# Attention with sigmoid scores and a token-mixing MLP: sums over both halves of the tensor array in one bank, under a new order

## The chip, the cores and the metric

The kernel runs on one core of one Trainium2 chip. The metric is the device time of one launch in microseconds, the median of several runs. The core has five engines that run side by side: TensorE (PE, matmuls and transposes into PSUM), VectorE (DVE), ScalarE (ACT), GpSimd (POOL) and SyncE (SP), which here only issues DMAs. PSUM has eight banks of 512 float32 per partition, 128 partitions.

## The reference

```python
def _attn_ref(q, k, v):                      # q, k, v: (8, 12, 448, 64)
    scores = scale * np.matmul(q, k.transpose(0, 1, 3, 2)) - np.log(S)
    attn = 1.0 / (1.0 + np.exp(-scores))
    return np.matmul(attn, v)

def _moe_ref(x, w_q, w_k, w_out):            # x: (8, 448, 768), from the heads side by side
    wq = x @ w_q                             # (8, 448, 64)
    wk = x @ w_k
    W_tok = scale * np.einsum('bsd,btd->bst', wq, wk)
    mixed = np.einsum('bst,btd->bsd', W_tok, x)
    return np.maximum(mixed, 0.0) @ w_out    # (8, 448, 768)
```

The scores pass through a sigmoid instead of a softmax, so no row sums are needed. The second part is linear in the token sums: the kernel forms tmp = wk^T x (64 by 768) first and then mixed = wq tmp, and never builds the 448 by 448 matrix W_tok.

## The kernel before, in words

**Attention.** The eight sequences with twelve heads each make 24 quads of four heads; quad n belongs to sequence u = n // 3. The 448 tokens of a head are split in seven blocks of 64. One scores step (function scores, line 307) takes one block: four matmuls, one on each 64 by 64 quarter of the array, put 2 x 448 scores on all 128 partitions of two neighbouring banks, and one sigmoid on ACT (L316) reads both banks and writes a bfloat16 buffer at. There are 24 x 7 = 168 such steps. A values step (L333) is four more matmuls; seven of them add up to one quad of x, transposed, which a copy (L342, or L340 in two pieces) brings to the buffers xt.

**What feeds it.** q, k and v are loaded as float32 by SP, cast to bfloat16 mostly on POOL (L192, L209, L215), and q and k are transposed, on DVE (L245, L269, L276) or on PE (L229, L237) with a copy (L294, L299). A ring of eight load buffers makes each load wait for the cast of the load eight places before it. ORDER (line 688) lists the loads; a dot moves a cast to DVE, a capital to ACT. w0 in it is the load of w_q and w_k, and w1 and w4 are the two loads of w_out, issued by POOL at line 653.

**The token MLP of a sequence.** x is transposed back on PE (tr_x: L355 with the whole array, L371 in quarters). W steps form wq and wk (mlp_wqk: L408 whole, L396 in quarters). N transposes wk (L423). U forms tmp (mlp_tmp, L437, or mlp_tmp_tiled, L452). M forms mixed and applies the relu (mlp_mix: L490, or L476 for the sequences of groups 1 and 2, whose 448 columns are laid out as 2 x 256; relu at L461 on ACT, L463 on DVE). O multiplies by w_out: out_chunk (L603, whole array, 128 tokens by 384 columns), out_pair (L522, quarters, for groups 1 and 2) and out_halves (L562, quarters). A group is two sequences; mxs[w] holds the mixed values of group w.

**Two halves of the array.** A quarter is one half of the rows (which part of the inner sum it takes) by one half of the columns (which partitions of a bank it writes). When the inner sum is split over the two row halves, each half sums into its own bank, and the two partial sums must be added. L396, L452 and L562 do that: a copy of one bank to SBUF (L403, L456, L567) and an add of the other on DVE (L404, L457, L568). out_pair avoids it in another way: each row half computes another block of tokens over the whole inner sum, in its own bank, for which it needs every row of w_out on both halves of the partitions. A second, swapped copy of w_out is made by twelve DMAs (the C steps, line 848).

**What sets the order.** Every engine runs its instructions in the order in which the program gives them; nothing reorders them. The program's order is written out by hand or by a planner: PLAN (line 132) is a string with one letter per step (S scores, P values, q and k the transposes of a quad, x, W, N, U, M, O as above, I an out_halves step, F a filling matmul, digits a cast; lower or other letters choose the engine or the form). BANKS (line 67) gives, step by step, the PSUM bank or the pair of banks that each step takes. After a step's matmuls, the copy or the sigmoid that reads its banks is issued, and the next step that is given those banks waits for it.

## Time and profile before

| what | value |
|---|---|
| time, median of 3 runs | 181.61 us (181.6 to 182.2) |
| the profiled execution's own time | 181.22 us |
| its span, first to last instruction | 179.4 us |
| busy: PE, ACT, DVE, POOL | 169.1, 158.9, 143.0, 124.2 us |
| PE weight loads busy | 115.5 us |
| mean granted clock of TensorE | 0.997 |
| bytes moved by DMA | 47.29 MB, 264 GB/s over the span |

The profile is one execution of the program, taken by the hardware profiler. Times are counted from the start of the span. L311 is line 311 of the kernel. A row of the chain gives start, length and the line that held the end at that time. A group row gives busy time, mean duration of one instruction in ns, then the idle time of the engine just before such instructions and what ended it. Matmuls overlap, so the mean duration of one (its whole way through the array) is longer than the step from one to the next; the step is what a stream costs. A row of a stretch gives the busy time of each engine in it, the granted clock and the DMA share.

### The profile page before, as it was taken

Reading aid. Unit: us, or ns where it says so; the run is one execution under the profiler, and the core shown is the slowest. Engines: PE = TensorE matmul, PEld = TensorE weight load, DVE = VectorE, ACT = ScalarE, POOL = GpSimd, SP = SyncE. Lnnn points to the kernel's source line nnn. Section 1 sums busy time; section 2 is a strip of 40 time slices with the busy share of each in tenths; the row PEclk is TensorE's granted clock in tenths of the full one; section 3 lists DMA queues with packets and bytes.
Section 4 is the critical chain, followed back from the end, with each engine's and each line's share of the span. In section 5 each row is a group of like instructions: output and inputs, shape, how many; then the busy total and the mean of one; then the engine's idle time right before and its main releaser. Section 6 shows DMA issues by size and latency. Waiting matters only on the chain.

```text
span 179.4 us, 7848 instructions
## 1 busy us (share of the span) xinstructions
PE 169.1 (94%) x3412; PEld 115.5 (64%) x3412; DVE 143.0 (80%) x223; ACT 158.9 (89%) x208; POOL 124.2 (69%) x169
## 2 busy tenths in 40 slices
PE   7888899889999999999999999999999999999990
PEld 7334545444674555755667788787888788888560
DVE  3447899998988897989999989979799885868351
ACT  4699999999999999999999999999999989967310
POOL 1286899998999999999999989879979810010000
PEclk9999999999999999999999999999999999999998
DMA  5999999999999998899996999959597432505876
GB/s 166 338 398 391 326 383 377 285 305 365 335 309 406 334 287 280 249 319 384 306 325 174 303 313 302 331 207 274 130 325 219 115 89 49 137 4 128 207 195 175
DMA packets 24914, 47.29 MB, mean 264 GB/s; under 512 B 3888, under 2 KB 18480, under 8 KB 24880
## 3 DMA queue, kind: packets, MB, share of 16 engines
q1 hardware_dynamic: 23600, 44.64, 76.9%
q0 software_dynamic: 800, 1.18, 3.6%
q10 hardware_dynamic: 480, 0.98, 1.5%
q8 instruction: 26, 0.43, 1.0%
q14 instruction: 8, 0.07, 0.1%
HBM read 35.78 MB, written 11.01 MB: 261 GB/s over the span
## 4 chain that ended last, share of the span: by engine, by line
PE 76%; ACT 15%; DMA 4%; SPq 1%; issue 1%; POOL 1%; DVE 0%
PE banks L311 16%; ACT at L316 15%; PE banks L522 15%; PE banks L333 14%; PE banks L603 13%; DMA k<-in_k_dram 4%; PE banks L562 3%; PE banks L408 3%; PE banks L371 2%; PE banks L396 2%; PE banks L355 2%; PE banks L452 2%; PE banks L476 1%; PE banks L490 1%; PE banks L437 1%
## 5 line engine op out<-in xcount | busy, mean ns | idle before, releaser
L316 ACT ACTIVATE at<-banks 128x896 bf16<-128x896 f32 x168 | 139.9, 951 | 2.9 <-PE banks L311 2.3
L311 PE MATMUL banks<-qk 64*64 64x448 bf16 x672 | 62.6, 357 | 3.7 <-ACT at L316 1.7
L333 PE MATMUL banks<-at,v 64*64 64x448 bf16 x672 | 47.3, 350 | 0.7 <-ACT at L316 0.7
L311 PEld LDWEIGHTS <-qk 64*64 64x64 bf16 x672 | 26.3, 105 | 21.4 <-issue 13.5
L522 PE MATMUL banks<-wout,mx 64*64 64x384 bf16 x672 | 36.3, 323 | 0.0
L333 PEld LDWEIGHTS <-v 64*64 64x64 bf16 x672 | 24.8, 106 | 6.7 <-issue 1.8
L342 DVE CAST xt<-banks 128x896 bf16<-128x896 f32 x22 | 23.7, 1083 | 2.4 <-PE banks L333 2.0
L522 PEld LDWEIGHTS <-mx 64*64 64x64 bf16 x672 | 23.2, 107 | 3.9 <-issue 0.2
L603 PE MATMUL banks<-wout,mx 128*128 128x384 bf16 (+1 forms) x138 | 24.4, 320 | 0.0
L192 POOL CAST qk<-k 128x896 bf16<-128x896 f32 x19 | 22.7, 1194 | 1.4 <-DMA k<-in_k_dram 1.0
L192 POOL CAST qk<-q 128x896 bf16<-128x896 f32 x18 | 21.5, 1193 | 2.5 <-DVE qk L276 1.4
L463 DVE TENSOR_SCALAR mx<-banks 128x1024 bf16<-128x1024 f32 (+3 forms) x22 | 21.3, 970 | 1.9 <-PE banks L476 0.7
L209 POOL CAST v<-v 128x896 bf16<-128x896 f32 x22 | 20.6, 950 | 1.4 <-DMA v<-in_v_dram 0.9
L603 PEld LDWEIGHTS <-mx 128*128 128x128 bf16 x138 | 12.3, 98 | 9.7 <-issue 3.2
L161 POOL COPY swap<-qk 32x448 uint32<-32x448 uint32 x28 | 15.5, 554 | 2.3 <-DVE qk L192 0.7
L276 DVE STREAM_TRANSPOSE qk<-qk 128x448 f32<-128x448 f32 x28 | 17.0, 628 | 0.1
L164 POOL COPY qk<-qk 32x448 uint32<-32x448 uint32 x28 | 15.8, 566 | 1.6
L167 POOL COPY qk<-swap 32x448 uint32<-32x448 uint32 x28 | 15.4, 552 | 1.6
L245 DVE STREAM_TRANSPOSE qk<-qk 32x448 f32<-32x448 f32 x24 | 15.3, 636 | 0.6
L405 POOL COPY wq<-wqk 64x448 bf16<-64x448 bf16 x3 | 1.7, 554 | 15.7 <-DVE wqk L404 15.7
L636 DVE COPY o<-banks 128x384 f32<-128x384 f32 x12 | 6.6, 554 | 5.7 <-PE banks L603 5.3
L636 ACT COPY o<-banks 128x384 f32<-128x384 f32 x9 | 4.4, 490 | 7.1 <-PE banks L603 6.6
(87 smaller groups left out, 207.9 us busy)
## 6 DMA issues: line engine op xcount, KB each, us to landing
q<-in_q_dram SPq DMA_DIRECT2D x24, 448.0 KB, 6.6
v<-in_v_dram SPq DMA_DIRECT2D x24, 448.0 KB, 6.6
k<-in_k_dram SPq DMA_DIRECT2D x23, 448.0 KB, 7.6
out_dram<-o SPq DMA_DIRECT2D x50, 192.0 KB, 4.2
wout<-in_moe_w_out_dram POOLq DMA_DIRECT2D x2, 576.0 KB, 11.7
wout<-wout SPq DMA_DIRECT2D x12, 96.0 KB, 5.6
out_dram<-o ACTq DMA_DIRECT2D x4, 192.0 KB, 3.2
k<-in_k_dram SPq DMA_DIRECT2D x1, 256.0 KB, 4.8
```

The source lines that it names most:

```text
L161: eng.tensor_copy(out=z[lo], in_=w[hi, 0])
L164: eng.tensor_copy(out=w[hi, 0], in_=w[lo, 1])
L192: COPY[e](out=f[:, :, "qk".index(nm)].rearrange("p e i d y -> p e y i d"), in_=ld.pop((nm, n)).rearrange("p (y i e d) -> p e y i d", y=2, ...
L209: COPY[e](out=t16.rearrange("p b i d -> p (b i d)"), in_=ld.pop((nm, n)).rearrange("p b x -> p (b x)"),)
L276: nc.vector.transpose(out=qk[n][:, t].rearrange("p t i n -> p (t i n)").bitcast(F32), in_=w)
L311: nc.tensor.matmul(sc[HALF[h], g, 0:S], qk[n][HALF[g], h, 1, i, :], qk[n][HALF[g], h, 0].rearrange("p i n -> p (i n)"), start=True, stop=True,
L316: inst = nc.scalar.activation(at, sc[:, :, 0:S], ACTF.Sigmoid, bias=attn_bias, scale=attn_scale)
L333: nc.tensor.matmul(ps[HALF[g], h, 0:S], ld["v16", n][HALF[h], g, i, :], ats[n, i][HALF[h], g, :], start=(i == 0), stop=(i == NI - 1),)
L342: read(fb, COPY[eng](out=xt(u, j)[:, :, 0:S], in_=ps[:, :, 0:S]))
L463: inst = nc.vector.tensor_scalar(dst, ps, moe_scale, 0.0, ALU.mult, ALU.max)
L522: nc.tensor.matmul(ps[HALF[x], y, 0:NB], mx[HALF[y], u, b, 64 * (i - 3 * y) : 64 * (i - 3 * y) + 64], wout16[HALF[y], slot(y, b), x * NB : ...
L603: nc.tensor.matmul(ps, mxs[w][:, 2 * S * c + m * P : 2 * S * c + (m + 1) * P], wout16[:, c, w0:w1], start=(c == 0), stop=(c == NC - 1),)
```

## The change

The partial sums no longer meet in an add. In the three places where the inner sum is split over the row halves (wq and wk, tmp, and the output), the columns or token blocks are now split in two as well, one for each bank. In the first half of the step, row half y sums its part into bank y; in the second half, row half y sums its part of the other block into bank 1 - y, onto what the other row half has left there. At the end each bank holds a finished sum, and one copy over both banks brings it out. Between the halves no two row halves may write one bank at the same time, so TensorE waits until its own last matmul of the first half is done (change). PLAN places other steps between the two halves; a letter V is added for the second half of tmp.

With it out_pair, the second copy of w_out and its twelve DMAs go, and the 2 x 256 layout of groups 1 and 2. The pool of output tiles has four buffers instead of three, there are 20 buffers at instead of 16, and wout16 is half as large. PLAN, BANKS and ORDER are new throughout; the group of two sequences, the functions for scores, values and transposes, and the loads themselves are the same. By the built programs PE has 3546 matmuls instead of 3412, and 25 waits on its own matmuls: 3 for wq and wk, 4 for tmp, 18 for the output.

```diff
-    p_o = pool("o", 3)
+    p_o = pool("o", 4)
...
+    SYNC = mybir.DependencyInfo(mybir.DependencyClass.Sync, mybir.DependencyReason.DATA)
+    turned = {}
+
+    def change(key):
+
+        tc.add_manual_dep(
+            nc.tensor.nop().ins, turned.pop(key).ins.name, SYNC, reason="the halves of the array change banks",
+        )
...
-    wout16 = singles.tile([P, 2 * NC, D], BF16, name="wout16")
+    wout16 = singles.tile([P, NC, D], BF16, name="wout16")
...
-    at_bufs = [singles.tile([P, 2, S], BF16, name=f"at{n}") for n in range(16)]
+    at_bufs = [singles.tile([P, 2, S], BF16, name=f"at{n}") for n in range(20)]
...
     def mlp_wqk(u, c, tail, act, tiled):
...
         if tiled:
-            for y in range(2):
-                for x in range(2):
-                    nc.tensor.matmul(
-                        ps[HALF[x], y, 0:S], wqk16[HALF[y], c, 64 * x : 64 * x + 64],
-                        xt(u, c // 2)[HALF[y], c % 2, 0:S], start=(c == 0), stop=(c == NC - 1),
-                    )
+            z, j = divmod(c, NJ)
+            if c == NJ:
+                change("W")
+            for b in (2 * j, 2 * j + 1):
+                for y in range(2):
+                    for x in range(2):
+                        inst = nc.tensor.matmul(
+                            ps[HALF[x], y ^ z, 0 : S // 2], wqk16[HALF[y], b, 64 * x : 64 * x + 64],
+                            xt(u, j)[HALF[y], b % 2, (y ^ z) * S // 2 : (y ^ z) * S // 2 + S // 2],
+                            start=(z == b == 0), stop=(z == 1 and b == NC - 1),
+                        )
+            if c == NJ - 1:
+                turned["W"] = inst
             if c == NC - 1:
-                part = p_one.tile([P, S], F32, tag="wpart", name="wpart")
-                read(fb, COPY["s" if act else "v"](out=part, in_=ps[:, 0, 0:S]))
-                read(fb, nc.vector.tensor_tensor(out=w[:, 0:S], in0=ps[:, 1, 0:S], in1=part, op=ALU.add))
-                nc.gpsimd.tensor_copy(out=w2[HALF[1]], in_=w[HALF[0], 0:S])
+                src = ps[:, :, 0 : S // 2]
+                read(fb, nc.vector.tensor_copy(out=w[:, 0:S].rearrange("p (z s) -> p z s", z=2), in_=src))
...
-    def mlp_tmp_tiled(u, act):
+    def mlp_tmp_tiled(u, t, act):
...
+                z = r ^ t
                 for y in range(2):
-                    nc.tensor.matmul(
-                        ps[HALF[y], r, 0:NB], wkn[u][HALF[r], m, :], xns[u][HALF[r], m, y * NB : (y + 1) * NB],
-                        start=(m == 0), stop=(m == 3 - r),
+                    inst = nc.tensor.matmul(
+                        ps[HALF[y], z, 0:h], wkn[u][HALF[r], m, :],
+                        xns[u][HALF[r], m, y * NB + z * h : y * NB + z * h + h],
+                        start=(t == m == 0), stop=(t == 1 and m == 3 - r),
                     )
-        read(fb, COPY["s" if act else "v"](out=part, in_=ps[:, 0, 0:NB]))
-        read(fb, nc.vector.tensor_tensor(out=tmps[u], in0=ps[:, 1, 0:NB], in1=part, op=ALU.add))
+        if t == 0:
+            turned["T"] = inst
+            return
+        read(fb, COPY["s" if act else "v"](
+            out=tmps[u].rearrange("p (z x) -> p z x", z=2), in_=ps[:, :, 0:h],
+        ))
...
-    def out_pair(act, split):
...
-    def out_halves(act):
+    def out_halves(act, split):
...
+        z, h = divmod(part, 2)
+        if part == 2:
+            change("O")
         for c in range(3 * h, 3 * h + 3):
-            t0 = 2 * S * c + m * P + b * NP
             for y in range(2):
+                t0 = 2 * S * c + m * P + (y ^ z) * NP
                 for x in range(2):
-                    nc.tensor.matmul(
-                        ps[HALF[x], y, 0:NB], mxs[w][HALF[y], t0 : t0 + NP], wout16[HALF[y], c, x * NB : (x + 1) * NB],
-                        start=(c == 0), stop=(c == NC - 1),
+                    inst = nc.tensor.matmul(
+                        ps[HALF[x], y ^ z, 0:NB], mxs[w][HALF[y], t0 : t0 + NP],
+                        wout16[HALF[y], c, x * NB : (x + 1) * NB],
+                        start=(part == 0 and c == 0), stop=(z == 1 and c == NC - 1),
                     )
-        if h:
-            read(fb, COPY["s" if act else "v"](out=o[:, b], in_=ps[:, 0, 0:NB]), keep=True)
-            read(fb, nc.vector.tensor_tensor(out=o[:, b], in0=ps[:, 1, 0:NB], in1=o[:, b], op=ALU.add), keep=True)
+        if part == 1:
+            turned["O"] = inst
...
+        if split:
+            for b in range(2):
+                read(fb, COPY["vs"[b]](out=o[:, b], in_=ps[:, b, 0:NB]), keep=True)
+        else:
+            read(fb, COPY["s" if act else "v"](out=o, in_=ps[:, :, 0:NB]), keep=True)
...
     ORDER = (
-        "q1 k1 k2 q2 q3 v0 w2 k3 v1 k4 q4 v2 w0 k5 q5 w1 v3 W5 v4 q6 k6 w4 k7 v5 q7 v6 q8 k8 k9 "
+        "q1 k1 v0 .q2 q3 k2 k3 v1 w0 q4 W3 v2 k4 v3 k5 w6 q5 q6 k6 k7 v4 w1 q7 w4 v5 k8 v6 q8 v7 "
...
-        elif kind == "C":
-            for y in range(2):
-                nc.sync.dma_start(out=wout16[HALF[y], NC + c, :], in_=wout16[HALF[1 - y], c, :])
```

More of the change, by code (lines that the diff above doesn't have):

```diff
@@ L384, in tr_x @@
             read(fb, COPY["vs"[g] if tail else eng](out=dst, in_=src))
-    wkn, tmps, mxs = {}, {}, {}
+    wkn, tmps, mxs, pt = {}, {}, {}, {}
     pw = {}
@@ L441, in mlp_tmp @@
         read(fb, COPY["s" if act else "v"](out=tmps[u], in_=ps))
-    def mlp_tmp_tiled(u, act):
-        tmps[u] = p_one.tile([P, NB], BF16, tag="tmp", name="tmp")
-        part = p_one.tile([P, NB], F32, tag="upart", name="upart")
-        fb, ps, _ = bank2()
+    def mlp_tmp_tiled(u, t, act):
+        h = NB // 2
+        if t == 0:
+            tmps[u] = p_one.tile([P, NB], BF16, tag="tmp", name="tmp")
+            pt[0] = bank2()
+        else:
+            change("T")
+        fb, ps, _ = pt[0]
         for m in range(4):
@@ L845 @@
             mlp_wqk(*divmod(c, NC), tail, t in "wl", t in "Ll")
-        elif kind == "C":
-            for y in range(2):
-                nc.sync.dma_start(out=wout16[HALF[y], NC + c, :], in_=wout16[HALF[1 - y], c, :])
         elif kind == "N":
@@ L851 @@
         elif kind == "U":
-            (mlp_tmp_tiled if t in "Tt" else mlp_tmp)(c, t in "ut")
+            tiled[c] = t if t in "Tt" else None
+            if tiled[c]:
+                mlp_tmp_tiled(c, 0, False)
+            else:
+                mlp_tmp(c, t == "u")
+        elif kind == "V":
+            if tiled[c]:
+                mlp_tmp_tiled(c, 1, tiled[c] == "t")
         elif kind == "M":
```

110 lines of the change are left out of this document (27 added, 83 removed), and 28 rows, old and new, of tables (BANKS, ORDER).

## The prediction

> **What bounds the kernel now.** I read four views in this order: the busy times of the engines in stretches of the span, the chain that ended last, the groups by line and shape, and the timeline of single engines where a latency was wanted.
>
> ```profile
> core 0: us, PE busy (x) PEld busy (x) DVE busy (x) ACT busy (x) POOL busy (x), PEclk, DMA share, GB/s
> 10.00:40.00 30.00, 26.36 (x510) 14.05 (x511) 26.28 (x36) 29.91 (x38) 26.68 (x33) 1.00 1.08 351
> 40.00:70.00 30.00, 29.57 (x538) 16.84 (x534) 26.80 (x41) 29.31 (x37) 27.66 (x39) 1.00 1.01 336
> 70.00:100.00 30.00, 30.00 (x513) 19.40 (x511) 26.84 (x39) 29.43 (x39) 28.42 (x38) 1.00 0.88 292
> 100.00:130.00 30.00, 29.92 (x731) 24.20 (x732) 26.39 (x40) 29.39 (x39) 26.08 (x37) 1.00 0.83 263
> 130.00:150.00 20.00, 20.00 (x552) 16.51 (x546) 17.57 (x23) 19.48 (x25) 12.29 (x18) 1.00 0.57 169
> 150.00:165.00 15.00, 15.00 (x444) 12.89 (x436) 10.52 (x21) 12.46 (x22) 0.56 (x1) 1.00 0.34 83
> ```
>
> Two engines stand at their limit. ACT is busy 29.91 us of the 30 between 10 and 40 us and, adding the rows, 137.52 of the 140 us from 10 to 150: it idles 2.48 us there. PE has gaps until 40 us and then 124.49 busy us of 125 up to 165. A busy PE need not be one that streams at its full rate, so I looked at single runs of matmuls in the chain.
>
> ```profile
> 11.49 27.67 ACT at L316 x34
> ...
> 46.46 1.08 PE banks L603 x6
> 47.55 0.31 PE banks L311 x4
> ...
> 52.86 0.57 PE banks L333 x12
> ...
> 57.12 0.77 PE banks L437 x8
> ...
> 80.09 0.98 PE banks L603 x6
> ...
> 100.40 0.45 PE banks L355 x8
> ...
> 102.64 0.57 PE banks L452 x14
> ...
> 111.49 0.49 PE banks L522 x12
> ...
> 158.94 0.25 PE banks L371 x32
> ```
>
> The chain runs through 34 sigmoids from 11.49 to 39.16 us (27.67 / 34 = 0.814 us each) and from there over PE. The runs repeat: four matmuls on the quarters of the array take 0.57 / 3 = 0.19 us for 448 columns and 0.49 / 3 = 0.163 us for 384; a matmul on the whole array takes 0.98 / 6 = 0.163 us for 384. Width sets the price, and nothing is left between neighbours of one shape. What is left lies at a change of shape: six L603 matmuls take 1.08 us behind quarters against 0.98 behind another whole-array line, and four L311 matmuls behind them 0.31 against 0.19. A switch of shape so costs 0.10 to 0.12 us, and I take 0.11. So from 40 us on the end moves with PE's work, and ACT stands right behind it with 2.5 us of room.
>
> **The change part by part, PE.** I counted matmuls and switches in the built order of both kernels.
>
> - Output projection: quarter matmuls of 384 columns go from 816 (L522 and L562) to 864, whole-array ones (L603) from 138 to 126. That is +48 x 0.49/12 = +1.96 and -12 x 0.163 = -1.96: nothing.
> - Mixing: groups 1 and 2 lose the padding to 512 columns. Twelve steps of eight 256-column matmuls become steps of four 448-column ones. The first kind takes 0.21 us, from start to the next line's start:
>
> ```profile
> 95.10 0.30 PE L476 MATMUL banks<-wq,tmp 64*64 64x256 bf16 x2
> ...
> 95.31 0.68 PE L522 MATMUL banks<-wout,mx 64*64 64x384 bf16 x12
> ```
>
>  12 x (0.19 - 0.21) = -0.24 us.
> - The sum over tokens (tmp): one tiled step fewer (14 matmuls of 384 columns, 0.57 us; the other four keep their columns in 28 half-wide matmuls), one untiled step more (eight L437 matmuls, 0.77 less its switch = 0.66): +0.09.
> - The tiled projections to wq and wk keep their columns in twice as many matmuls: 0. Bounds: nothing shows a 224 or 192 column matmul, but 64, 256, 384 and 448 columns cost 0.25/32, 0.21/8, 0.49/12 and 0.57/12 us, so 7.8, 26, 41 and 47.5 ns, in proportion to width within 15%. Half-wide ones could thus be dearer by at most 15% of about 5.7 us, 0.8; I take 0, since the neighbours on both sides (64 and 256 columns) are near proportion.
> - Transposes of x: one quad goes from L355 to L371: 0.25 - 0.45 = -0.20.
> - Switches of shape: 68 become 63: -5 x 0.11 = -0.55.
>
> Sum: -0.24 + 0.09 - 0.20 - 0.55 = -0.90 us.
>
> The row of 32 transposes in 0.25 us is one matmul in 7.8 ns: on quarters of the array no floor shows above that. The Trainium skill, "TensorE: Matmul & The Clock Gate", section "Wait — 56ns, not 53.3ns?", speaks against narrow matmuls: start to start never falls below about 25 ns, however few the columns. By it the sum would be, as an estimate from that page, some 0.7 us higher; the trace does not bear it out.
>
> **The waits on PE's own matmul.** There are 25: three for wq and wk, four for tmp, 18 for the output halves. Both halves of the array may not write one bank at once, so the first matmul after the change waits for the last one before it. No row shows PE waiting for itself, so I bound it. Uncovered, the price is the matmul's time past its own streaming, and the way from a signal to the next matmul:
>
> ```profile
> L522 PE MATMUL banks<-wout,mx 64*64 64x384 bf16 x672 | 36.3, 323 | 0.0
> ```
>
> ```profile
> 161.01 0.81 PE L452 MATMUL banks<-xn,wkn 64*64 64x384 bf16 x14
> 161.86 0.48 ACT L456 COPY upart<-banks 128x384 f32<-128x384 f32 x1 [0.81 <-PE banks L452]
> 162.38 0.56 DVE L457 TENSOR_TENSOR tmp<-banks,upart 128x384 bf16<-128x384 f32 x1
> ...
> 162.99 0.11 PEld L490 LDWEIGHTS <-tmp 64*64 64x64 bf16 x4
> 163.05 0.35 PE L490 MATMUL banks<-wq,tmp 64*64 64x448 bf16 x2
> ```
>
> 323 - 163 = 160 ns past streaming, 40 ns from PE's end (161.82) to a reader, and 110 ns from a finished producer (162.94) to PE's next matmul: 0.27 us together with the larger of the two signals. Bounds: 0 and 25 x 0.27 = 6.8 us. In the built order other PE work stands in each of the 25 places: in one it is a single step of scores (0.19 us), in one 32 transposes (0.25), in the other 23 two steps or more (0.35 and up). That covers 0.27 us in 23 places and leaves 0.08 + 0.02 = 0.1 us. I take 0.1. Behind each waiting instruction stand scores that ACT needs, which is why the cover counts.
>
> **What else moves.** DVE loses the adds that joined the two halves; it is not the bound (26.8 of 30 us at its fullest), so I cost its relief at nothing, and at nothing the larger pools. SP loses the twelve copies of w_out (the diff's C steps); by the windows above PE has 0.5 us of gaps in the 125 us from 40 us on, so there is nothing to win there either. ACT gets more before its last sigmoid:
>
> ```profile
> L636 ACT COPY o<-banks 128x384 f32<-128x384 f32 x9 | 4.4, 490 | 7.1 <-PE banks L603 6.6 <-ACT mx L461 0.4 <-ACT at L316 0.2
> L461 ACT ACTIVATE mx<-banks 128x448 bf16<-128x448 f32 x6 | 3.2, 564 | 0.2 <-PE banks L490 0.2
> L461 ACT ACTIVATE mx<-banks 128x1024 bf16<-128x1024 f32 x2 | 2.0, 1018 | 0.0
> L535 ACT COPY o<-banks 128x768 f32<-128x768 f32 x2 | 1.6, 798 | 0.6 <-PE banks L522 0.6
> L340 ACT CAST xt<-banks 128x448 bf16<-128x448 f32 x2 | 1.1, 561 | 0.0
> L209 ACT CAST v<-v 128x896 bf16<-128x896 f32 x1 | 0.9, 930 | 0.0
> ```
>
> Before: nine 384-wide copies (4.41), one 768-wide (0.80), one L340 (0.56), two 1024-wide relus (2.04), two narrower ones (priced at the 448 row: 1.13), one v cast (0.93): 9.9 us. After: eight copies of 384 (3.92), one of 768 (0.80), three L340 (1.68), three relus of 448 (1.69), one v cast (0.93), and three of 896 columns out of the banks, for which I take 0.93 between 0.80 and 1.02 (2.79): 11.8 us. So +1.9 us, against 2.48 us of idle: the room shrinks to 0.6 us but is not gone.
>
> **Sum.** -0.90 + 0.1 = -0.8 us against the profiled execution's own 181.22 us (179.4 of span and 1.8 around it): 180.4. That execution lies 0.4 us under the median, and I forecast for the median: 181.6 - 0.8 = 180.8; as the lighter DVE can only release banks sooner, I round to **180.7**.
>
> **The rivals.**
>
> A, ACT eats the gain (the change shortens PE, and nothing follows). If ACT keeps its 2.48 us of idle, its last sigmoid starts 1.9 us later.
>
> ```profile
> 6.44 5.97 ACT L316 ACTIVATE at<-banks 128x896 bf16<-128x896 f32 x7 [0.80 <-PE banks L311]
> ...
> 152.20 3.35 ACT L316 ACTIVATE at<-banks 128x896 bf16<-128x896 f32 x4
> ```
>
> These are the first seven and the last four. Behind the last scores PE's order gets shorter: 48 fewer quarter matmuls of the output (-1.96), 32 fewer transposes (-0.25), four more values matmuls (+0.19), an untiled tmp for a tiled one (+0.09) and two switches (+0.22): -1.7 us. So +1.9 - 1.7 = +0.2: 181.8. For it: ACT is at 98% for 140 us. Against it: part of ACT's idle time is waiting for late scores, which come sooner.
>
> B, both streams close up. If ACT's idle time halves (-1.2), A becomes -1.0, and if it vanishes -2.3: about 179.5. For it: a lighter DVE; against it: two engines that both stand at their limit rarely interlock without gaps.
>
> C, slower: a load that comes late where ACT has no room. The place is the third quad: its k is now the ninth load and must be cast on POOL, transposed on PE and copied by DVE before the 15th sigmoid.
>
> ```profile
> 9.14 0.93 POOL L215 CAST k<-k 128x896 bf16<-128x896 f32 x1 [0.23 <-DMA k<-in_k_dram]
> ...
> 13.86 0.93 POOL L209 CAST v<-v 128x896 bf16<-128x896 f32 x1 [0.19 <-DMA v<-in_v_dram]
> ```
>
> ```profile
> 17.37 1.09 DVE L299 COPY qk<-banks 128x1792 bf16<-128x1792 bf16 x1 [0.87 <-PE banks L229]
> ```
>
> The ninth load is there at about 13.8 us (the v cast waited for it), the cast ends at 14.8, transposes and copy (0.3 + 1.09, and 0.2 of signals) at 16.4. The seventh sigmoid ends at 12.41 (6.44 + 5.97) and starts, by the chain, at 11.49, so the 15th is due at 11.49 + 8 x 0.814 = 18.0, and its scores 0.4 us ahead, at 17.6. The room is 1.2 us; what is later goes to the end one for one, since ACT is full until 150 us. It decides from 1.2 + 0.8 = 2.0 us late; at 3.2 us late: 181.6 - 0.8 + 2.0 = 182.8. For it: POOL waited 0.2 us for the load in both rows, so nothing is in hand there. Against it: 1.2 us of room.
>
> D, slower: the cover of the self-waits fails, say because PE's queue holds nothing ahead of the wait. 25 x 0.27 - 0.9 = +5.9: 187.5; it turns the sign from four open places of 25. Against it: the order above.
>
> E, narrow matmuls have a floor. If a half-wide one costs no less than the 256-column one (26 ns by its row), 144 x 2.2 + 112 x 5.6 ns = 0.95 us are added and the gain is gone: 181.7. For it speaks no row, against it the transposes. This is the rule of the Trainium skill that is named above ("TensorE: Matmul & The Clock Gate").
>
> **How the numbers follow.** A measurement here can tell about 0.5%, 0.9 us, from no change: faster is under 180.7, slower over 182.5. The forecast (from 179.9 to 181.3) has 0.42, split 0.25 faster and 0.17 same, as its middle lies at the bound; A 0.20 (same); B 0.14 (faster); C 0.15 (0.12 slower, 0.03 same); D 0.07 (slower); E 0.02 (same). Faster 0.39, same 0.42, slower 0.19. The range takes in B, the forecast, A, E and C up to some 3.5 us late, and leaves out D and the far ends of B and C: 179.2 to 183.3.
>
> **What would show it.** PE's work: a run of twelve output matmuls at 0.49 us on both sides of a change, and 63 switches at 0.1. The self-waits: PE idle before the changed line, under its releaser PE, summing to about 0.1 us; several us would be D. A: ACT's idle time between 10 and 150 us as before, with the last sigmoid later than 154.7 us and PE's tail behind it 1.7 us shorter. C: sigmoids 14 to 22 with gaps that a load or a cast ended. E: half-wide matmuls at 25 ns each. I would be wrong altogether if PE waited for DVE or POOL between 40 and 150 us, where before it hardly waits.

## The result, and the profile after

The changed kernel takes 183.41 us (median of 22 runs, 181.86 to 185.69), the kernel before in the same comparison 181.89 us (22 runs, 180.73 to 184.08). The ratio is 1.0084 with a 95% interval from 1.0057 to 1.011: slower by about 1.5 us, where 0.9 us less was forecast. The medians are over all runs, the ratios leave disturbed runs out, so a ratio need not be the quotient of its medians. The profiled execution of the changed kernel took 184.2 us, with a span of 182.4 us.

First the busy times in the same stretches as before:

```profile
core 0: us, PE busy (x) PEld busy (x) DVE busy (x) ACT busy (x) POOL busy (x), PEclk, DMA share, GB/s
10.00:40.00 30.00, 25.65 (x531) 14.26 (x531) 24.20 (x34) 29.84 (x37) 26.27 (x32) 1.00 1.03 357
40.00:70.00 30.00, 28.51 (x555) 18.21 (x553) 27.00 (x40) 29.04 (x37) 27.95 (x38) 1.00 0.92 277
70.00:100.00 30.00, 29.91 (x588) 18.70 (x577) 27.17 (x41) 29.41 (x38) 28.13 (x38) 1.00 0.93 323
100.00:130.00 30.00, 29.67 (x671) 21.36 (x669) 23.83 (x35) 29.83 (x41) 25.93 (x37) 1.00 0.82 260
130.00:150.00 20.00, 18.98 (x560) 15.91 (x562) 14.66 (x22) 18.19 (x23) 10.11 (x16) 1.00 0.55 148
150.00:165.00 15.00, 15.00 (x462) 12.02 (x456) 8.68 (x17) 13.75 (x22) 0.55 (x1) 1.00 0.35 83
```

Between 40 and 150 us PE idles 1.49 + 0.09 + 0.33 + 1.02 = 2.93 us; before it was 0.43 + 0 + 0.08 + 0 = 0.51. These 2.4 us and a first sigmoid at 7.08 instead of 6.44 us (a difference that comes and goes: 6.2 to 7.1 us in the other profiles of the new order, but for the one with more warm-ups) add up to the 3.0 us by which the span is longer. It is no full account: the stretch from the first to the 43rd sigmoid also takes 34.59 us instead of 34.13, and PE has less work by shape. The chain that ended last names two places:

```profile
35.21 0.57 issue
35.78 0.90 POOL wout L633
36.67 1.09 POOL qk L200
37.77 14.37 DMA wout<-in_moe_w_out_dram
52.18 0.68 PE banks L536 x12
...
111.15 0.38 PE banks L319 x8
...
113.17 0.49 PE banks L536 x12
...
123.55 0.38 PE banks L411 x16
...
129.67 1.35 issue
131.02 0.32 PE banks L379 x17
```

**L, a late load.** Before, the chain ran through 34 sigmoids up to 39 us and then over PE. Now it runs through a load: the second half of w_out is issued by GpSimd at 37.77 us (at 30.86 before), lands 14.37 us later (12.81 before), and PE's output matmuls wait for it. **F, a late packet of instructions.** At 129.67 us PE stands still for 1.35 us and waits for nothing that the profile shows, in the middle of a run of 32 transposes (15 before the gap, 17 behind it). The timeline of PE shows both in brackets:

```profile
52.18 0.68 PE L536 MATMUL banks<-wout,mx 64*64 64x384 bf16 x12 [0.84 <-DMA wout<-in_moe_w_out_dram]
```

```profile
129.31 0.36 PE L379 MATMUL banks<-ident,xt 64*64 64x64 bf16 x15
131.02 0.32 PE L379 MATMUL banks<-ident,xt 64*64 64x64 bf16 x17 [1.35 <-issue]
```

Why instructions? PE's instructions reach it by DMA, in packets. The view of the DMA queues has a row for that queue, first of the kernel before, then of the changed one:

```profile
q8 instruction: 26, 0.43, 1.0%
```

```profile
q8 instruction: 27, 0.44, 1.0%
```

0.44 MB in 27 packets is some 16 kB each. By the built program the transpose behind the gap is PE's instruction number 4803, and 4803 = 18 x 256 + 195. The other gaps marked "issue" that are quoted below sit at numbers with that rest too. So I take a packet for 256 instructions (64 bytes each), and its first one for a border. PE has 7101 instructions now against 6833.

### The profile page after: what moved, and what is told of

Read it like the earlier page. It is cut to its first block, busy times and chain, and to the rows that moved or that the text cites. A ratio compares the mean times of both kernels' runs of the same rounds, so it can differ in the third digit from the quotient of the medians.

```text
span 182.4 us, 8090 instructions
## 1 busy us (share of the span) xinstructions
PE 169.7 (93%) x3546; PEld 114.2 (63%) x3546; DVE 134.8 (74%) x212; ACT 160.2 (88%) x209; POOL 120.6 (66%) x165
## 4 chain that ended last, share of the span: by engine, by line
PE 67%; DMA 20%; POOL 6%; DVE 2%; issue 2%; SPq 1%; POOLq 0%; DVEq 0%
PE banks L536 19%; PE banks L319 13%; PE banks L341 12%; PE banks L583 11%; DMA wout<-in_moe_w_out_dram 8%; DMA v<-in_v_dram 4%; DMA k<-in_k_dram 4%; DMA w<-in_moe_w_k_dram 4%; POOL qk L200 3%; PE banks L503 2%; PE banks L427 2%; PE banks L411 2%; PE banks L379 2%; PE banks L363 1%; PE banks L455 1%
## 5 line engine op out<-in xcount | busy, mean ns | idle before, releaser
L536 PE MATMUL banks<-wout,mx 64*64 64x384 bf16 x864 | 45.8, 323 | 0.8 <-DMA wout<-in_moe_w_out_dram 0.8
L319 PEld LDWEIGHTS <-qk 64*64 64x64 bf16 x672 | 27.4, 105 | 20.1 <-issue 9.7
L536 PEld LDWEIGHTS <-mx 64*64 64x64 bf16 x864 | 28.8, 107 | 7.3 <-issue 1.4
L341 PEld LDWEIGHTS <-v 64*64 64x64 bf16 x672 | 23.1, 106 | 7.4 <-issue 1.5
L492 DVE TENSOR_SCALAR mx<-banks 128x896 bf16<-128x896 f32 (+1 forms) x23 | 20.4, 902 | 4.7 <-PE banks L503 4.5
L350 DVE CAST xt<-banks 128x896 bf16<-128x896 f32 x17 | 18.5, 1087 | 6.2 <-PE banks L341 6.1
L583 PE MATMUL banks<-wout,mx 128*128 128x384 bf16 (+1 forms) x126 | 21.6, 319 | 0.0
L200 POOL CAST qk<-k 128x896 bf16<-128x896 f32 x17 | 20.3, 1195 | 1.0 <-DVE qk L284 0.4
L175 POOL COPY qk<-swap 32x448 uint32<-32x448 uint32 x28 | 15.9, 569 | 1.6
L551 DVE COPY o<-banks 128x768 f32<-128x768 f32 x11 | 10.5, 950 | 4.7 <-PE banks L536 2.9
L392 DVE COPY xn<-banks 128x1024 bf16<-128x1024 bf16 (+1 forms) x15 | 9.7, 647 | 4.0 <-PE banks L379 3.7
```

The lines of the kernel that those rows point to most:

```text
L175: eng.tensor_copy(out=w[lo, 1], in_=z[lo])
L200: COPY[e](out=f[:, :, "qk".index(nm)].rearrange("p e i d y -> p e y i d"), in_=ld.pop((nm, n)).rearrange("p (y i e d) -> p e y i d", y=2, ...
L319: nc.tensor.matmul(sc[HALF[h], g, 0:S], qk[n][HALF[g], h, 1, i, :], qk[n][HALF[g], h, 0].rearrange("p i n -> p (i n)"), start=True, stop=True,
L341: nc.tensor.matmul(ps[HALF[g], h, 0:S], ld["v16", n][HALF[h], g, i, :], ats[n, i][HALF[h], g, :], start=(i == 0), stop=(i == NI - 1),)
L350: read(fb, COPY[eng](out=xt(u, j)[:, :, 0:S], in_=ps[:, :, 0:S]))
L492: inst = nc.vector.tensor_scalar(dst, ps, moe_scale, 0.0, ALU.mult, ALU.max)
```

## The experiments

Three theories about the 1.5 us. **L**: the late w_out load. **F**: the late packet. **Cover**: part of the PE work that was saved lay ahead of 40 us, where ACT sets the pace, so nothing is gained there. A rival to all of them is that the self-waits or the half-wide matmuls cost more than priced. The times of before differ a little from chip to chip, so each ratio is taken on one chip; the changed kernel's is 1.0084, and ratios, not medians, are what to compare across paragraphs. The diffs of ORDER show only the part of the line that changes.

**The load earlier, and the waits without cover.** The first edit moves the two w_out loads in ORDER:

```diff
-  v3 k5 w6 q5 q6 k6 k7 v4 w1 q7 w4 v5
+  v3 w1 k5 w6 q5 w4 q6 k6 k7 v4 q7 v5
```

> The changed kernel with one edit: in the list of loads the two loads of w_out are issued by POOL some 8 us earlier. Theory L (the loads of w_out come late: in the changed kernel's profile PE stands 0.84 us and ACT 0.76 us at the first output step, behind a load that took 14.4 us): that idle time is gone, the stretch from 45 to 60 us is 0.8 to 1.2 us shorter, and the time lies some 1.0 us under the changed kernel, 182.2 to 182.6. Rival W (the waits of PE on its own matmuls make the loss): time as the changed kernel, 183.2 to 183.6. Rival F (a packet of PE's instructions comes late, 1.35 us once in the profile): as the changed kernel on average, with a gap of PE at an instruction number that leaves the rest 195 when divided by 256.

Measured: 183.87 us, ratio 1.0122 [1.0075, 1.0168]. The wait at 52 us is gone from the profile (PE is busy 10.00 of the 10 us from 50 to 60), the gap at 130 us stays with 0.89 us, and the time doesn't fall, where some 1.0 us less was expected. The 35th sigmoid comes 0.5 us late under this order, so the edit isn't a clean test of L.

The second edit puts each `change` right behind the last matmul that it waits for, so that nothing covers the wait.

```diff
-            if c == NJ:
-                change("W")
...
             if c == NJ - 1:
                 turned["W"] = inst
+                change("W")
```

> The changed kernel with the 25 waits of PE on its own matmul set right behind that matmul, so that no other PE work covers them. By the prediction's price each costs 0.27 us, and where PE is the bound they add up: 25 x 0.27 = 6.8 us, some 190 us; those that fall where ACT is the bound cost less, so 188 to 190. Rival W (the waits cost much already where they stand): only a little is added, 183.5 to 185.

Measured: 188.3 us, ratio 1.035 [1.0297, 1.0403]. At a bared wait mostly 0.38 to 0.40 us pass from the start of the last 384-column matmul to the next start, where four such matmuls take 0.16 us without a wait; behind half-wide ones it is 0.30 to 0.32 us against 0.08 to 0.10. So a wait costs some 0.24 us, an estimate from these starts. The waits view names PE as its own releaser, up to 0.5 us a time; then that view of the changed kernel, which has one such row:

```profile
PEld L319 <- PE banks L532: 3.1, 7, 0.4
PEld L501 <- PE banks L532: 2.2, 5, 0.4
```

```profile
PEld L476 <- PE banks L476: 0.2, 1, 0.2
```

Uncovered, the waits cost 4.6 us more than the changed kernel took on the same chip (183.71, below); covered, the changed kernel's profile has 0.2 us of them. They aren't the cause.

**Both kernels again.** To see what is constant, the changed kernel and the one before ran unchanged.

> The changed kernel itself, a second profile. Theory L: the stand at the first output step shows again, 0.5 to 1.2 us, at the same place. Rival F: a gap of PE behind a late packet of instructions shows in some executions and at varying places; the 1.35 us at 129.6 us need not come again. Time 183.0 to 184.0.

> The kernel before, a second profile. Theory L: no wait of PE for the loads of w_out, which are issued 15 us ahead of their first use. Rival F: gaps of PE of 0.3 us and more at the same rest of the instruction number, if any. The first sigmoid starts within 0.7 us of the 6.4 us of the first profile, which tells how far the 0.65 us later start of the changed kernel's profile is its own.

Measured: 183.71 us, ratio 1.007 [1.0019, 1.012], and 180.91 us for the one execution of the kernel before. The second profile of the changed kernel has the wait for w_out again, larger, and two gaps for want of instructions, at numbers 4803 and 5315:

```profile
52.28 0.68 PE L536 MATMUL banks<-wout,mx 64*64 64x384 bf16 x12 [1.71 <-DMA wout<-in_moe_w_out_dram]
```

```profile
130.59 0.32 PE L379 MATMUL banks<-ident,xt 64*64 64x64 bf16 x17 [0.62 <-issue]
141.33 0.54 PE L341 MATMUL banks<-at,v 64*64 64x448 bf16 x5 [1.67 <-issue]
```

The places recur, the sizes vary. That this makes single executions spread by over 3 us is not shown: those of the kernel before spread as much, and in its two profiles PE has neither that wait nor a gap over 0.35 us after 40 us.

**The borders moved by 96 instructions.** 48 more warm-up matmuls (with their weight loads 96 instructions) ahead of everything:

```diff
-    for _ in range(32):
+    for _ in range(80):
```

> The changed kernel with 80 instead of 32 warm-up matmuls, which run while PE waits for the first loads (about 2.7 us of 4): 96 more PE instructions ahead of everything else, and nothing else changed. Theory F (PE's instructions arrive in blocks of 256, and a block that is used up too fast leaves PE waiting for the next): the block borders stand 96 instructions earlier in the work, where three blocks hold only 2.3 to 3.4 us of PE work; gaps without a releaser stand again at instruction numbers with the rest 195 by 256, at other places of the work than 129.6 us, and are larger: 185 to 188 us. Theory L and rival W (late load of w_out, waits on own matmuls): nothing changes but the start, 183.2 to 184.0.

Measured: 184.92 us, ratio 1.0169 [1.0105, 1.0232]. The warm-ups start the first sigmoid 2 us late (8.64 us). The gap in the transposes is gone: no row of PE's timeline from 119 to 145 us ends in "issue". Less these 2 us (0.011 of the ratio) it is 1.006, within the noise of the changed kernel's 1.0084. The larger gaps that the expectation names elsewhere don't come: 0.25 us at 163.39 us is all.

**The inner projections as before.** The tiled wq and wk steps and tmp go back to full-width matmuls in two banks, with a copy and an add (seven waits and 128 matmuls fewer); once with the w_out loads late, once with them early as in the first edit, and the early loads alone once more.

```diff
-                            ps[HALF[x], y ^ z, 0 : S // 2], wqk16[HALF[y], b, 64 * x : 64 * x + 64],
+                        ps[HALF[x], y, 0:S], wqk16[HALF[y], c, 64 * x : 64 * x + 64],
...
+                read(fb, nc.vector.tensor_tensor(out=w[:, 0:S], in0=ps[:, 1, 0:S], in1=part, op=ALU.add))
```

> The changed kernel with two of its three new sums undone: wq and wk, and tmp, are again summed in full-width matmuls in two banks and joined by a copy and an add; the output halves, the order and the banks stay. 128 fewer matmuls, 256 fewer PE instructions (a whole block), 7 of the 25 waits gone, the same columns, 7 copies and adds more on DVE. Theory F: the gap at 129.6 us shrinks or goes, 0.5 to 1.2 us less than the changed kernel: 182.3 to 183.0. If only the late w_out counts: 183.2 to 183.6, or a little more for the adds.

> The last kernel with the loads of w_out issued earlier as well. Theories L and F together: both gaps gone, 181.3 to 182.0, at the kernel before or a little under it. Theory F alone: as the last kernel.

> The changed kernel with the loads of w_out issued earlier, once more with more rounds, since six timed runs showed no gain (183.87) while the profile showed the stand at the first output step gone (2.33 us of PE gaps between 40 and 70 us against 3.55 and 4.2). Theory L: 182.3 to 182.9 in the median. If the gap that goes there only comes back later (ACT or instruction packets): 183.4 to 184.0, with gaps after 70 us larger by about 1 us than in the changed kernel's profiles.

Measured: 183.3 us, 1.0076 [1.0038, 1.0115]; 183.15 us, 1.0077 [1.0039, 1.0115]; 183.6 us, 1.0118 [1.0062, 1.0174]. So the half-wide matmuls and the waits are about even with the full-wide ones and their adds. With 256 PE instructions fewer the first two profiles have no gap for want of instructions from 119 to 145 us (the third has 1.37 us at 129.67 us), yet the load's wait is there again in the first of the three:

```profile
52.49 0.68 PE L522 MATMUL banks<-wout,mx 64*64 64x384 bf16 x12 [1.22 <-DMA wout<-in_moe_w_out_dram]
```

The second has neither L nor that gap, was expected at 181.3 to 182.0 us, and is no faster than the first. This speaks against L and F as the whole cause in the median.

**One projection as before, and fillers in pieces.** A smaller shift: only group 5's wq and wk in full-width matmuls, 48 instructions fewer ahead of 130 us. And a shift without delay: each of the ten filler matmuls of 512 columns is cut into six, 100 instructions more.

```diff
+        if tiled and u == 5:
...
+                        ps[HALF[x], y, 0:S], wqk16[HALF[y], c, 64 * x : 64 * x + 64],
...
+            return
```

```diff
-            nc.tensor.matmul(bank1()[1], zeros[:, 0:P], zeros, start=True, stop=True)
+            filled = bank1()[1]
+            for y in range(6):
+                cut = slice(86 * y, min(86 * y + 86, 512))
+                nc.tensor.matmul(filled[:, cut], zeros[:, 0:P], zeros[:, cut], start=True, stop=True)
```

> Only the projection to wq and wk of group 5 goes back to full-width matmuls in two banks, a copy and an add: 24 matmuls (48 instructions of PE, with their weight loads) and one self-wait fewer, ahead of 130 us. Late packet of PE's instructions: the gap of 1.35 us in the middle of the transposes at 131 us shrinks or is gone, because PE reaches the border 48 instructions later in its stream and with more time since the last packet; 0.6 to 1.0 us less than the changed kernel, 182.4 to 182.8. Saved PE work lies under ACT's cover, and that is all: no difference, 183.4. DVE's add and the extra bank cost: 0 to 0.3 us more, 183.4 to 183.7.

> The changed kernel with each of the filler matmuls of 512 columns ahead of the first scores cut into six: the same columns, 100 instructions of PE more, all borders between packets of PE's instructions fall 100 instructions earlier in the work, and the start isn't delayed. Late packet: the gap in the transposes at 131 us moves to a place where PE is slower between two borders and is hidden there; 0.6 to 1.3 us less, 182.1 to 182.8. Cover of ACT alone: no difference, 183.4 within 0.3. If the borders that the fillers move fall badly elsewhere: up to 184.5, with an issue gap at another place of the stream.

Measured: 183.67 us, 1.0078 [1.0031, 1.0126], and 184.07 us, 1.0159 [1.0112, 1.0206]. In both profiles the "issue" gap in the transposes at 131 us is gone. The first has the largest wait for w_out so far, 2.12 us at 52.55 us. The second has none, but new gaps, each at a border (instructions 1731, 1987 and 2755):

```profile
51.38 0.35 PE L319 MATMUL banks<-qk 64*64 64x448 bf16 x1 [0.80 <-issue]
57.58 0.64 PE L536 MATMUL banks<-wout,mx 64*64 64x384 bf16 x9 [0.17 <-issue]
78.06 0.38 PE L319 MATMUL banks<-qk 64*64 64x448 bf16 x3 [0.75 <-issue]
```

Moving the borders moves the gaps; it doesn't end them.

**More PE work, early and late.** Twelve scores steps are issued twice, the second time over the first.

```diff
+        for _ in range(2 if 20 <= len(sigmoids) < 32 else 1):
...
+        for _ in range(2 if 100 <= len(sigmoids) < 112 else 1):
```

> The changed kernel with the scores of the 21st to 32nd step issued twice (the second time over the first, so the output is the same): 12 x 0.19 = 2.3 us more work for PE while ACT is dense, 20 to 33 us. Theory that PE's work ahead of 40 us lies under ACT's cover: the sigmoids of these steps keep their 0.81 us and the time rises by under 0.8 us, to 183.4 to 184.2. The prediction's ledger, by which every microsecond of PE's work reaches the end: 2.3 us more, 185.7.

> The same repetition for the 101st to 112th step, around 100 to 112 us, again 12 x 0.19 = 2.3 us more work for PE. There PE is the bound by the windows: both theories expect all of it at the end, 185.5 to 185.9 (less by up to 0.8 if the 96 more instructions also move the border of the late packet at 131 us to a better place, 184.7). If it also stays under 184.2, ACT's cover reaches the whole program and the ledger fails everywhere.

Measured: 185.66 us, 1.0241 [1.0169, 1.0313], and 183.65 us, 1.0133 [1.0082, 1.0185], four runs each. The early repetition, then the late one, in the stretch from 20 to 34 us:

```profile
20.00:34.00 14.00, 13.19 (x252) 7.08 (x247) 11.34 (x18) 13.24 (x17) 13.38 (x17) 1.00 1.03 385
```

```profile
20.00:34.00 14.00, 12.60 (x290) 7.33 (x290) 12.43 (x20) 14.00 (x19) 13.30 (x19) 1.00 1.00 371
```

ACT loses 0.76 us of its 14 to 2.3 us of extra PE work, and after 43 sigmoids, counted from the first, the early kernel is 35.29 - 33.93 = 1.36 us behind. So by the trace 0.9 to 1.5 us of 2.3 were covered (2.3 less 1.36 and less 0.76): the cover is partial. The measured times don't show it: by the ratios, against 1.0084, the early repetition costs some 2.9 us, more than its work, and the late one, expected at its full 2.3, some 0.9. Behind the early repetition the profile has a gap of 1.09 us at 78.26 us for want of instructions, where the changed kernel has none. The late repetition, beside the changed kernel's trace, costs 1.9 us from the 97th to the 115th sigmoid and gets 1.5 of it back from the 139th to the 145th: its 96 instructions move the border out of the transposes at 131 us, and the gap there is gone. But 183.65 us also lies under the 184.2 at which the expectation gives up the ledger of PE's work everywhere. A plain addition of work and a shift of borders can't be had apart here, so Cover stays open.

**The loads behind q5, alone and with the shift; later loads; the kernel before with cut fillers.**

In ORDER, first behind q5 (once alone and once with group 5 as before), then later:

```diff
-  q5 q6 k6 k7 v4 w1 q7 w4 v5
+  q5 w1 w4 q6 k6 k7 v4 q7 v5
```

```diff
-  q5 q6 k6 k7 v4 w1 q7 w4 v5
+  q5 q6 k6 k7 v4 q7 v5 w1 w4
```

The kernel before gets the same cut of its filler matmuls as above.

> The changed kernel with both w_out loads issued on GpSimd right behind the cast of q5, at about 30 us instead of 35.8 and 37.8; nothing else moves ahead of q5 and k5, so the 36th sigmoid isn't late as it was in the earlier version. L (PE and ACT wait at 52 us for w_out): the gap at 52 us is gone, 1.0 us less than the changed kernel, 182.2 to 182.6, with the late packet at 131 us left. F alone: no difference, 183.4.

> Both edits: the loads behind q5, and the projection to wq and wk of group 5 in full-width matmuls. L and F together are the cause: 181.6 to 182.3, the time of before within 0.3%, both gaps gone and PE's last matmul at about 175 us. If the early part (PE idle under ACT up to 43 sigmoids, 0.9 us more than before) is a loss too and not only missing gain: 182.5. Neither L nor F: 183.4 to 183.7.

> The changed kernel with both w_out loads issued behind the cast of v5, about 3 us later than in the changed kernel. L: the loads land about 2 to 3 us later, PE waits at 52 us for that much longer, and the time rises by 1.5 to 3 us, 184.9 to 186.4. If the wait at 52 us is in the profiled execution only or is made good later: 183.4.

> The kernel before with each of its filler matmuls cut into six, which moves all borders between packets of PE's instructions by 100. If a random place of the borders costs about what it costs in the changed kernel, and the order of before has a good one: 0.5 to 1.3 us more, 182.4 to 183.2, with an issue gap in PE's stream that before doesn't have. If late packets cost nothing at before's density of instructions (6833 against 7101): no difference, 181.9.

Measured: 183.57 us, 1.0088 [1.005, 1.0125]; 182.6 us, 1.0044 [1.0002, 1.0086]; 189.11 us, 1.0293 [1.0209, 1.0377]; 182.51 us, 1.0023 [0.9986, 1.0059].

The later loads are the strongest sign for L. They were issued at 37.34 and 38.2 us, only 1.6 and 0.4 us later than in the changed kernel (my 3 us was wrong), back to back; the second took 15.9 us, landed 2.0 us later than in the changed kernel, and PE waited 4.06 us. The measured time rose by some 3.8 us by the ratios (5.7 between the medians, which are of two chips):

```profile
54.20 1.18 PE L536 MATMUL banks<-wout,mx 64*64 64x384 bf16 x12 [4.06 <-DMA wout<-in_moe_w_out_dram]
```

The wait isn't all of it. From 50 to 60 us, behind the two longest waits (4.06 us here, 2.12 in the kernel with only group 5 as before, above), TensorE's mean granted clock (the third number from the end) is 0.66 and 0.83; in the changed kernel's second profile, with a wait of 1.71 us, it stays at 1.00:

```profile
50.00:60.00 10.00, 5.94 (x72) 3.93 (x71) 3.34 (x5) 3.64 (x5) 9.28 (x15) 0.66 0.95 335
```

```profile
50.00:60.00 10.00, 7.88 (x142) 5.79 (x139) 5.26 (x8) 6.48 (x9) 9.28 (x15) 0.83 0.93 336
```

```profile
50.00:60.00 10.00, 8.29 (x188) 6.37 (x184) 7.24 (x10) 8.33 (x12) 9.29 (x14) 1.00 0.95 347
```

For the same work, between the 43rd and the 97th sigmoid, PE is busy 48.80 and 47.60 us there, and 45.82 in the changed kernel's first profile. So the low clock adds 3.0 and 1.8 us to the wait itself. The kernel with the later loads also has a packet's gap of 1.91 us at 136.37 us.

With the loads behind q5 that wait is gone, and 1.11 us at 129.39 us is left of F; with group 5 as before, 0.37 us of it:

```profile
129.39 0.32 PE L379 MATMUL banks<-ident,xt 64*64 64x64 bf16 x17 [1.11 <-issue]
```

```profile
129.34 1.46 PE L547 MATMUL banks<-wout,mx 64*64 64x384 bf16 x29 [0.37 <-issue]
```

The two differ by 0.97 us in the measured median, the way that F would have it, but their intervals overlap. And the kernel before, its borders moved, has in its profile what it never had:

```profile
122.00 0.76 PE L396 MATMUL banks<-xt,wqk 64*64 64x448 bf16 x11 [1.71 <-issue]
```

```profile
138.37 0.35 PE L311 MATMUL banks<-qk 64*64 64x448 bf16 x1 [1.11 <-issue]
```

These sit at instructions 4291 and 5059. So the gaps are no property of the new matmuls: the order of before has borders in harmless places. Its measured time hardly moves, though: the profile is of one of its longest executions (185.21 of 182.04 to 185.55 us), so such gaps need not be in the median one.

**The place behind k7.** Behind q5 the loads (1.67 us on GpSimd) push the casts of q6 and k6 back, PE waits 0.42 and 0.47 us for them (in the kernel with group 5 as before), and the 35th sigmoid comes 0.83 us late. (The expectation puts this down to the copy of wq, which was late too; the trace names the casts.) So they stand behind k7 in the last two.

```diff
-  q5 q6 k6 k7 v4 w1 q7 w4 v5
+  q5 q6 k6 k7 w1 w4 v4 q7 v5
```

> Both edits as in the run before, but the w_out loads stand behind the cast of k7, after GpSimd's copy of wq, issued at 34.9 and 35.8 us instead of 30.8 and 31.7. L and F explain the slowdown and the late copy explains what was left: 181.6 to 182.2, within 0.3% of before, no gap over 0.3 us at 52 or 131 us and the 35th sigmoid on time. If the loads then still land after 51 us (14 to 16 us after their issue, as in the kernels with late loads): a gap of 0.3 to 0.8 us at 51 us and 182.4 to 183. If the early part under ACT's cover costs by itself: 182.6 as before.

> The place behind k7 alone, on the changed kernel: L smaller or gone, no late copy of wq, the late packet at 131 us (F) stays. With F at 1.0 us by the pair of runs behind q5: 182.6 to 183.1. If F's 1.0 was chance: 181.8 to 182.3, as the run beside it.

Measured: with group 5 as before 182.65 us, 1.0056 [1.0024, 1.0089]; without 183.16 us, 1.0075 [1.0034, 1.0117]. No wait for w_out is left in either. In the first the 35th sigmoid is on time, PE idles 0.05 us from 40 to 70 us, and what is left of its idle time is mostly F:

```profile
100.00:130.00 30.00, 29.30 (x677) 21.92 (x679) 24.46 (x36) 28.62 (x38) 24.27 (x36) 1.00 0.81 253
130.00:150.00 20.00, 19.82 (x561) 16.19 (x557) 13.81 (x19) 19.35 (x25) 10.56 (x16) 1.00 0.56 148
```

```profile
128.93 1.46 PE L547 MATMUL banks<-wout,mx 64*64 64x384 bf16 x29 [0.67 <-issue]
```

From start to start of its matmuls PE takes 0.99, 0.45 and 0.31 us at three borders here (at 128.9, 143.1 and 147.1 us). Its span is still 1.0 us longer than that of the kernel before, and PE's idle time from 40 to 150 us only 0.5 us longer (1.02 against 0.51): the other half has no name here.

**What this adds up to.** Both edits together may bring back up to half: 1.0044 and 1.0056 against 1.0084, but 1.0077 where all inner projections are as before, and all three intervals overlap the changed kernel's. One edit alone brings nothing that can be measured: without L 1.0122, 1.0118, 1.0088 and 1.0075, with F shifted alone 1.0078 and 1.0076. That the load and the packets stall PE is shown by the profiles, and for the load by its later place too; how much either costs the median execution isn't, and so the cause of the 1.5 us is shown for the profiled executions only.

Profiled executions with the late load mostly lie above the median of their kernel (up to 2.3 us), those with the early one 0.4 to 1.0 us below it, so the wait may be longer in the profiled executions than in the others. No trace shows an unprofiled one, and that stays open. Known of each execution is its mean granted clock: it is 0.991 or less, as in the two profiles above, in 25 of 152 executions of the new order (all 6 with the later loads, 2 of the changed kernel's first 22) and in 1 of 105 of the kernel before. So a halved clock goes with the new order, but it is too rare to make the difference of the medians. No version here beats the kernel before.

## Why the prediction was wrong, point by point

- **The prices of PE's work** held. Twelve output matmuls take 0.49 us, sixteen half-wide L411 ones 0.38 us (23.8 ns each, half of 47.5), twelve of 192 columns 0.25 us (L476, 20.8 ns), eight of 448 columns in the mixing 0.38 us. Rival E's price, 26 ns for a half-wide matmul, is refuted by these rows. The floor of about 25 ns that the Trainium skill gives in "TensorE: Matmul & The Clock Gate", section "Wait — 56ns, not 53.3ns?", is not, for one quarter: the starts come in groups of four, one on each quarter, and the groups stand 83 ns apart for 192 columns (0.25 us / 3) and 31 for 64 (0.25 / 8). Only the mean over the four quarters falls below 25 ns. By these prices and the counts of the prediction PE's work is some 0.85 us less than before, against 0.90 predicted:

```profile
123.55 0.38 PE banks L411 x16
...
134.00 0.25 PE banks L476 x12
...
166.77 0.38 PE banks L503 x8
```

- **The self-waits** held: 0.1 us predicted, one row of 0.2 us seen; the price of 0.27 us came out at some 0.24 where they were bared. Rival D didn't happen.
- **ACT's extra work** was sized right (copies of 896 columns at 0.93 us; measured 0.92 and 0.97), and it wasn't what decided:

```profile
L350 ACT CAST xt<-banks 128x896 bf16<-128x896 f32 x2 | 1.9, 971 | 0.0
...
L490 ACT ACTIVATE mx<-banks 128x896 bf16<-128x896 f32 x1 | 0.9, 919 | 0.0
```

 ACT idles 3.69 us from 10 to 150 us against 2.48, waiting where PE waits. The last sigmoid starts at 158.97 us, 4.4 us later and not A's 1.9; from there to the start of PE's last matmul it is 18.97 us against 20.33, so 1.4 us less, near A's 1.7.
- **"From 40 us on the end moves with PE's work"** is doubtful as a way to book the 0.9 us. Some of it may have been saved ahead of 40 us, where ACT is at 29.84 of 30. PE's busy time from 10 to 40 us falls by 0.71 us (26.36 to 25.65), but the first sigmoid starts 0.64 us later, and from the first to the 43rd it falls only from 29.79 to 29.68. The early repetition's trace has 0.9 to 1.5 of 2.3 us covered, its measured time none. How much of the gain was lost in this way isn't shown.
- **"What else moves"** is the step that failed worst. I counted the twelve copies of w_out that go, and costed the loads at nothing. The two loads of w_out themselves had moved behind v4 and q7 in ORDER, 9.3 and 6.9 us later, against a use at 50 to 51 us and landings 11.1 and 14.4 us after the issue (10.7 and 12.8 before). PE's 0.5 us of gaps after 40 us, which I read as "nothing to win there", said nothing of what there was to lose: they became 2.93 us in the profile, 0.84 of them for this load, which is nearly the whole gain that was forecast.
- **The supply of instructions** had no term at all. Twice as many half-wide matmuls at the same streaming cost are 268 instructions of PE more, and a gap of this kind stood in the trace of before, at instruction 1731, where I passed it over (the row below). In the profile of the changed kernel it is 1.35 us, and with the load's 0.84 it makes the larger part of the 2.4 us of idle time that came new; whether both do as much in the median execution stays open:

```profile
54.31 0.57 PE L311 MATMUL banks<-qk 64*64 64x448 bf16 x7 [0.35 <-issue]
```

- **Rival C** named the right kind, a load that comes late where there is no room, and its 182.8 us was the nearest forecast, partly by luck: the place was wrong. Its own place, early in the program, does show up, one cast further on: in four of 17 profiles of the new order the load of k3 holds GpSimd up, v1's cast stands behind it, and PE waits for v1 for 0.94 to 1.44 us. The kernel with the loads behind k7 alone has it:

```profile
16.38 1.19 POOL L200 CAST qk<-k 128x896 bf16<-128x896 f32 x1 [1.65 <-DMA k<-in_k_dram]
17.69 0.94 POOL L217 CAST v<-v 128x896 bf16<-128x896 f32 x1
```

```profile
18.68 0.96 PE L341 MATMUL banks<-at,v 64*64 64x448 bf16 x8 [1.44 <-POOL v L217]
```

 In the three profiles of the order of before it doesn't occur. It is perhaps part of the spread, and of what both edits leave.

## What to carry to other kernels

Where an order is planned anew, list every load that changes its place, with its issue, its usual way to landing and its first use; that column is worth more than a second look at the matmuls. With two engines at their limit a late arrival is dear: two loads that were issued 0.4 and 1.6 us later cost some 3.8 us here: their way grew longer too, PE came to wait 4.06 us, and its granted clock was half for a while behind the wait. A gap seen in one profile need not be in the median execution: weigh it by the measured times before you call it the cause. And splitting a matmul costs nothing in streaming here but doubles its instructions, which come to the engine on a queue of their own.

## What the runs showed of the hardware

- **Packets of PE's instructions.** I set the packets of queue q8 beside PE's instructions in 20 traces, 520 borders. A packet starts up to 4.4 us after PE has crossed the border before it, takes 0.9 to 2.2 us (mostly 1.0), and PE never crosses the next border earlier than 1.21 us after its end. Where PE stood at a border for want of instructions, the crossing came 1.24 to 1.57 us after the packet: 1.47 us at 131.02 us in the changed kernel. So, as an estimate from these figures, a block of 256 instructions that PE passes in under some 3 to 6 us is at risk; in the dense stretch of half-wide matmuls and transposes ahead of that gap it passed one in 4.3 us (120.8 to 125.1).
- **The way of the w_out loads**, 576 kB each, took 7.7 us at the shortest (the first of the two behind q5, with group 5 as before) and 15.9 us at the longest (the second of the later ones). The second took 1.4 to 4.9 us longer than the first, but for the three profiles with the loads earliest, where it was up to 0.6 us shorter.
- **A bank change without cover** costs PE some 0.24 us.
- **The granted clock behind a wait.** With the later loads PE waits 4.06 us up to 54.20 us, and its granted clock is 0.50 from 53.25 to 60.08 us; with only group 5 as before it waits 2.12 us up to 52.55 us, and the clock is 0.50 from 53.84 to 57.26 us. Behind the waits for w_out of 0.30 to 1.71 us in the other profiles it stays at 1.00. In two of the four profiles in which PE waits for v1 it is 0.50 for 3.41 us from 18.3 and 18.7 us on (waits of 1.44 and 0.94 us), in the other two not (1.15 and 1.00 us); so no single length of a wait decides.
